# Reordering the sum and gather work around one PSUM bank, and the first and last of 64 late jobs, in a retention, GLU and expert-mixture kernel

## The chip, the cores and the metric

The kernel runs on one core of one Trainium2 chip. The metric is the device time of one execution in microseconds (us), taken as the median of several runs; lower is better. In the profile the engines are PE (TensorE matmul), PEld (TensorE's weight loads, which overlap its matmuls), DVE (VectorE), ACT (ScalarE), POOL (GpSimd) and SP (SyncE, which here issues most DMAs).

## The reference

Three layers follow each other on 2304 tokens of 512 features: a retention (attention with a decaying mask and no softmax), a gated linear unit, and a mixture of 8 experts in which every token goes through every expert, weighted by a Sinkhorn-normalized matrix. Only the last layer matters here:

```python
def _moe2_ref(x, w_gate, w1, w2):        # x 2304x512, w1 8x512x1024, w2 8x1024x512
    logits = x @ w_gate
    P = np.exp(logits - logits.max())
    for _ in range(8):
        P /= P.sum(1, keepdims=True) + 1e-09
        P /= P.sum(0, keepdims=True) + 1e-09
        P *= N / E
    out = np.zeros((N, D))
    for e in range(E):
        h = np.maximum(x @ w1[e], 0.0)
        out += P[:, e:e + 1] * (h @ w2[e])
```

Each fp32 matrix operand is split into a high part `hi` (rounded to the matmul's type) and a rest `lo = x - hi`, and each product is computed as `hi*hi + hi*lo + lo*hi`, three matmuls.

## The kernel before

**Jobs.** The mixture is cut into 96 jobs: 3 units of 768 tokens, in each unit 8 experts, and in each expert 4 groups of 256 hidden features. The 32 jobs of unit 0 also prepare the weights and keep them in DRAM. The 64 late jobs (numbers 32 to 95, units 1 and 2) load them back. All engine queues run in the order in which the program is written; nothing reorders it.

**A late job.** Both layers of a job are done by a Strassen-like scheme of 7 block products with sums of blocks (A11, A12, A22, S1 to S4) in place of 8 products. A first-layer product (`block_product`) is 6 matmuls of 128x384, into the PSUM banks `px`, `py`, `pz` or `qz`. A second-layer step (`second`) is 3 matmuls, and 7 steps for each of two output halves `j`; they go into `qx`, `qy`, `qz` and a bank `shared_sums[j]` (the tiles `pv` and `e`). So a job issues 42 + 42 = 84 matmuls.

**The order within the loop.** The body of job `n` holds the first layer of job `n`, most of the second layer of job `m = n - 1`, and the last two second-layer steps (`c12` and `c21` for `j = 1`) of job `l = n - 2`, woven together. The second layer needs the parts of the hidden blocks of `m`: `high(m, S2)` is a cast on ACT, and `low(m, S2)` a subtraction on DVE or, for S3 and S4, on POOL (line 975). The results leave PSUM by `gather`, an addition `acc += bank` on DVE (line 989); the names `add_11`, `add_22`, `add_12`, `add_21` say which quarter. `add_12` empties `qy` and `add_21` empties `qz`.

In the order of each queue, the first half of a body is:

- PE: product A11 of `n` into `px`; `c12(l, 1)` into `qy`; `c21(l, 1)` into `qz`; product S2 of `n` into `py`; `first(m, 0)` into `qx`; `shared(m, 0)` into `pv`; product S1 of `n` into `qz`; `third(m, 0)`, which reads the parts of S2, into `qy`; `c11(m, 0)`, which reads the parts of A12, into `qx`; product A12.
- DVE, from the end of the body before: `h_blocks[1]` (line 1157), `add_22(m, 1)`, `low A11`, `add_11(m, 1)`, and then `low S1`, `low A12`, `add_12(l, 1)`, `add_21(l, 1)`, `low S2`.
- POOL: the four sums S1 to S4 of the hidden blocks (lines 1152, 1154, 1173, 1174), then `low S3` and `low S4`.
- ACT: `high S1, A12, S2`, the copy `py <- px`, `high S3`, the copy `pz <- py`, the copy `qy <- qx` (line 999, which overwrites the bank that `add_12` reads), `high S4`.

**Homes of the sums.** The blocks and sums of a job lie in `h_blocks` (the tile `a22_block` and `old[:, 0, 0]`) and `sums`, four pieces of `old`. `old` is `acc_d[:, :, :768]`, the place of unit 0's output, which the six DMAs of line 811 (issued by ACT, inside `outputs_of` of job 31) write out while job 32 (`opening` in the code) already runs.

**Change of unit and end.** At job 64 the generator `switch` splits the last operands of unit 2 (line 613 on DVE, in `split`), and at job 65 `add_shared` adds the shared banks into the output of unit 1 (line 1037), after which `finish_unit` transposes it piece by piece. After the loop the last steps of jobs 94 and 95 follow, then `finish_unit` for unit 2: for each of 6 chunks of 128 tokens four transposes, a copy from PSUM to a staging tile (two of these in turn, from ACT and DVE) and an output DMA from SP.

Of the kernel before, what the change touches and what calls it, by code (L numbers as in the profile page):

```python
# [39 lines left out]
T = 384  # L40
# [9 lines left out]
def retention_glu_experts(ctx: ExitStack, tc: tile.TileContext, a, out):  # L50
# [709 lines left out]
    def block_product(n, ps, w, name, start=False):  # L760
        s = w1_slots[n % 2]
        xh, xl = x_ops[jobs[n][0]][name]
        for k in range(2):
            kc = slice(k * 128, (k + 1) * 128)
            wh, wl = s[:, 0, w, kc], s[:, 1, w, kc]
            for i, (l, r) in enumerate(((wh, xh), (wh, xl), (wl, xh))):
                nc.tensor.matmul(  # L767
                    ps, lhsT=l, rhs=r[:, k, :], start=start and k == 0 and i == 0,
                    stop=k == 1 and i == 2, skip_group_check=True,
                )  # L770
# [170 lines left out]
    old = acc_d[:, :, :UNIT].rearrange("p k (h t) -> p k h t", t=T)  # L941
    h_blocks = [a22_block, old[:, 0, 0]]
    sums = [old[:, k, h] for k, h in ((1, 0), (0, 1), (1, 1), (2, 0))]
    T1, T2, T3, T4, B21, B22, B11 = range(7)

    def halves(p, i):
# [16 lines left out]
            nc.sync.dma_start(prob_b[e % 2], prob_kept[e, (u - 1) * UNIT:u * UNIT].partition_broadcast(128))  # L963

    def operand(n, i):
        return h_ops[n % 2][i], {A22: h_blocks[0], A12: h_blocks[1], A11: z[:, 1, :]}.get(i, sums[(i - S1) % 4])

    def high(n, *parts):
        for i in parts:
            (hi, _), x = operand(n, i)  # L970
            nc.scalar.copy(hi, x)  # L971

    def low(n, i, engine=None):
        (hi, lo), x = operand(n, i)
        (engine or nc.vector).tensor_sub(lo, x, f32(hi))  # L975
# [20 lines left out]
    def first(n, j):  # L996
        x, y, z, e = banks_of(n, j)
        second(n, j, A11, B11, x, start=True)
        nc.scalar.copy(y, x)  # L999
# [15 lines left out]
    def c12(n, j):  # L1015
        second(n, j, S4, B22, banks_of(n, j)[1])

    def c21(n, j):
        second(n, j, A22, T4, banks_of(n, j)[2])
# [7 lines left out]
    def add_12(n, j):  # L1027
        gather(n, 2 + j, 1, banks_of(n, j)[1])

    def add_21(n, j):  # L1030
        gather(n, j, 0, banks_of(n, j)[2])

    def add_shared(u):
        for j in range(2):
            for h in range(2):
                o = acc_d[:, 2 + j, u * UNIT + h * T:u * UNIT + (h + 1) * T]
                nc.vector.tensor_add(o, o, shared_sums[j])

    def finish_unit(u, banks, stages):
        for t in range(NCH):  # L1040
            ps = banks[t % len(banks)]
            tag, shape = stages[t % len(stages)]
            at = u * UNIT + t * 128
            for k in range(KD):
                nc.tensor.transpose(ps[:, k * 128:(k + 1) * 128], acc_d[:, k, at:at + 128], ident)
            st = ev.tile(shape, F32, tag=tag, name=f"st{u}_{t}").rearrange("p a b -> p (a b)")[:, :DM]
            if t % len(stages):
                nc.vector.tensor_copy(st, ps)
            else:
                nc.scalar.copy(st, ps)  # L1050
            nc.sync.dma_start(out[at:at + 128, :], st)
            yield
# [3 lines left out]
    for n, (u, e, g) in list(enumerate(jobs))[UJ:]:  # L1056
        opening = n == UJ
        m, l = n - 1, n - 2
        pb = prob_b[e % 2]
        load_w1(n + 1)  # L1060
        if u + 1 < NU and (e, g) == (E - 1, NPAIR - 3):
            switch = unit_operands(u + 1)
        ahead = u + 1 < NU and (e, g) in ((E - 1, NPAIR - 3), (E - 1, NPAIR - 2))
        turn = u + 1 < NU and (e, g) == (E - 1, NPAIR - 1)
        begins = (e, g) == (0, 0)
        if g == NPAIR - 1:
            load_probs(n + 1)

        block_product(n, px, 0, "A11", start=True)
        if not opening:  # L1070
            high(m, S2)
        nc.scalar.copy(py, px)  # L1072
        if not opening:
            high(m, S3)
            low(m, S1)
            low(m, A12)
        if begins:
            next(switch)
        if l >= UJ:
            c12(l, 1)  # L1080
            c21(l, 1)
            add_12(l, 1)
            add_21(l, 1)
            if jobs[l][1:] == (E - 1, NPAIR - 1):
                add_shared(jobs[l][0])
                finishing = finish_unit(jobs[l][0], [qx_all], [("xs", [128, 2, T])])
        load_w2(n)
        p5 = ev.tile([128, T], F32, tag="p5", name=f"p5_{n}")
        if opening:
            block_product(n, pv, 3, "S1", start=True)  # L1090
            nc.scalar.copy(p5, pv)
            next(ys)
            block_product(n, py, 4, "S2")
            nc.scalar.copy(pz, py)
            next(switch)
            next(ys)
        else:
            low(m, S2)
            block_product(n, py, 4, "S2")
            nc.scalar.copy(pz, py)  # L1100
            if turn or begins:
                next(switch)
            first(m, 0)
            high(m, S4)
            low(m, S3, nc.gpsimd)
            low(m, S4, nc.gpsimd)
            shared(m, 0)
            block_product(n, qz, 3, "S1", start=True)
            nc.scalar.copy(p5, qz)
            if ahead:  # L1110
                next(switch)
            third(m, 0)
            c11(m, 0)
            add_11(m, 0)

        block_product(n, px, 1, "A12")
        nc.vector.scalar_tensor_tensor(h_blocks[0], px, 0.0, pb[:, :T], ALU.max, ALU.mult)
        if turn:
            next(switch)
        if opening:  # L1120
            next(ys)
        else:
            next(finishing, None)
            c22(m, 0)
            add_22(m, 0)
            c12(m, 0)
            add_12(m, 0)
        high(n, A22)
        low(n, A22)

        block_product(n, pz, 5, "S3")
        z = ev.tile([128, 2, T], F32, tag="z", name=f"z{n}")
        nc.vector.tensor_add(z[:, 1, :], pz, p5)  # L1133
        if turn or ahead:
            next(switch)
        if opening:
            next(ys)
        else:
            first(m, 1)
            c21(m, 0)  # L1140
            add_21(m, 0)

        block_product(n, py, 2, "S4")
        nc.vector.tensor_add(z[:, 0, :], py, p5)
        z_2 = z.rearrange("p h t -> p (h t)")
        nc.vector.scalar_tensor_tensor(z_2, z_2, 0.0, pb, ALU.max, ALU.mult)  # L1146
        if opening:
            next(ys)
        else:
            third(m, 1)  # L1150
            shared(m, 1)
        nc.gpsimd.tensor_add(sums[0], z[:, 0, :], h_blocks[0])  # L1152
        high(n, A11)
        nc.gpsimd.tensor_sub(sums[1], sums[0], z[:, 1, :])

        block_product(n, pz, 6, "A22")
        nc.vector.scalar_tensor_tensor(h_blocks[1], pz, 0.0, pb[:, T:], ALU.max, ALU.mult)
        if opening:
            for _ in ys:
                pass  # L1160
            shared_all, shared_sums = pv_all, [pv, pac.tile([128, 512], F32, tag="ac", name="e1")[:, :T]]
            qx_all, qy, qz = (pac.tile([128, 512], F32, tag="ac", name=f"q{i}") for i in "xyz")
            qx, qy, qz = (q[:, :T] for q in (qx_all, qy, qz))
            for q in (qy, qz):
                nc.tensor.matmul(q, lhsT=sx[:, 0, 0, 0, :128], rhs=sx[:, 0, 0, 0, :], start=True, stop=True)
        else:
            c22(m, 1)
            add_22(m, 1)
        low(n, A11)
        if not opening:  # L1170
            c11(m, 1)
            add_11(m, 1)
        nc.gpsimd.tensor_sub(sums[2], z[:, 1, :], z[:, 0, :])
        nc.gpsimd.tensor_sub(sums[3], h_blocks[1], sums[1])
        high(n, S1, A12)

    n, l = len(jobs) - 1, len(jobs) - 2
    high(n, S2, S3)
    low(n, S1)
    low(n, A12)  # L1180
    c12(l, 1)
    add_12(l, 1)
    first(n, 1)
    c21(l, 1)
    add_21(l, 1)
    low(n, S2)
    first(n, 0)
    high(n, S4)
    low(n, S3, nc.gpsimd)
    low(n, S4)  # L1190
    for step in (shared, third, c11):
        for j in (1, 0):
            step(n, j)
            if step is c11:
                add_11(n, j)
    add_shared(NU - 1)
    for step, add in ((c22, add_22), (c12, add_12), (c21, add_21)):
        for j in (1, 0):
            step(n, j)
            add(n, j)  # L1200
    for _ in finish_unit(NU - 1, [shared_all, qx_all, px_all, py_all], [("xs", [128, 2, T]), ("z", [128, 2, T])]):
        pass


# [69 lines left out]
```

## Time and profile before

| what | us |
|---|---|
| median of 3 runs | 2132.06 (2130.42 to 2132.81) |
| the profiled execution's own time | 2136.81 |
| its span, first to last instruction | 2134.9 |
| PE busy / PEld busy in the span | 2058.7 / 1884.9 |
| DVE / ACT / POOL busy | 1480.1 / 860.3 / 846.5 |
| mean granted TensorE clock | 0.990 |

PE counts as busy from the start of a matmul to its modelled end, and these overlap, so its share hides short waits; the waits of PEld, which come when a weight load is held back, show them better. A row of a timeline gives start, length, engine, line, operation, output and inputs, and in square brackets how long the engine had been idle and what released it. In the profile's names `z` and `a_block` and `acc` are the homes of the hidden blocks and sums, `xhi` and `xlo` those of their parts.

### The profile page before, as it was taken

To read this page: it belongs to the slowest core of one execution; us is meant where nothing else is said; L and a number is where in the kernel's file an instruction comes from. 1 tells how busy PE (TensorE), PEld (TensorE's weight loads), DVE (VectorE), ACT (ScalarE), POOL (GpSimd) and SP (SyncE) were. 2 spreads that over 40 slices of the span, in tenths; PEclk is the share of its full clock that TensorE was granted. 3 is DMA by queue.
4 is the path that set the end of the run, shared out by engine and by line. 5 is a ranking of instruction groups with operands and counts; after the bars stand their busy time and mean duration, and the time that the engine had idled before them with its cause. 6 is when DMAs were issued, how large, how long until landed. Compare 5 with 4: busy or idle time off the path is not lost.

```text
span 2134.9 us, 30383 instructions
## 1 busy us (share of the span) xinstructions
PE 2058.7 (96%) x11526; PEld 1884.9 (88%) x11526; DVE 1480.1 (69%) x2323; ACT 860.3 (40%) x1649; POOL 846.5 (40%) x747
## 2 busy tenths in 40 slices
PE   8999999999998999999998999999999999999997
PEld 5688789889777899999998999999998999999997
DVE  6863775653579777777785777777776677777776
ACT  3443322221353544444444444444445444444443
POOL 3421542210043445555443353444464444444443
PEclk8999999999999999999999999999999999999999
DMA  6420220100056888888877666666665767666763
GB/s 219 158 87 1 79 70 30 60 30 1 1 197 252 290 295 306 310 300 307 301 282 294 245 253 245 250 248 247 251 236 221 273 230 272 223 258 232 270 227 129
DMA packets 112690, 436.58 MB, mean 204 GB/s; under 512 B 12297, under 2 KB 30473, under 8 KB 96161
## 3 DMA queue, kind: packets, MB, share of 16 engines
q1 hardware_dynamic: 110048, 432.72, 55.4%
q10 hardware_dynamic: 2496, 1.94, 0.3%
q8 instruction: 90, 1.47, 0.3%
q14 instruction: 56, 0.45, 0.1%
HBM read 312.40 MB, written 122.21 MB: 204 GB/s over the span
## 4 chain that ended last, share of the span: by engine, by line
PE 71%; DVE 20%; ACT 1%; DMA 1%; issue 1%; POOL 0%; DVEq 0%; SPq 0%; POOLq 0%; ACTq 0%
PE pz L767 9%; DVE xlo L975 9%; PE py L767 6%; PE px L767 6%; DVE acc L989 6%; PE qy L981 5%; PE gv L173 4%; PE gv L175 4%; PE gv L174 4%; PE qz L767 4%; PE y L174 4%; PE y L175 4%; PE y L173 4%; PE qx L981 3%; PE qz L981 3%; PE x L173 2%
## 5 line engine op out<-in xcount | busy, mean ns | idle before, releaser
L1152 POOL TENSOR_TENSOR acc<-z,a_block 128x384 f32<-128x384 f32 x64 | 64.9, 1015 | 509.2 <-DVE z L1146 481.7
L767 PE MATMUL py<-sx,w1s 128*128 128x384 f32 x1152 | 233.0, 337 | 6.0 <-ACT py L1072 5.8
L767 PEld LDWEIGHTS py<-sx,w1s 128*128 128x128 f32 x1152 | 203.7, 188 | 10.0 <-ACT py L1072 7.3
L767 PE MATMUL px<-xhi,w1s 128*128 128x384 f32 x640 | 188.9, 335 | 0.0
L971 ACT CAST xhi<-acc 128x384 fp32r<-128x384 f32 x320 | 158.1, 514 | 74.6 <-POOL acc L1152 35.4
L975 DVE TENSOR_TENSOR xlo<-acc,xhi 128x384 fp32r<-128x384 f32 x193 | 178.1, 949 | 2.7 <-ACT xhi L971 2.6
L975 POOL TENSOR_TENSOR xlo<-acc,xhi 128x384 fp32r<-128x384 f32 x127 | 148.9, 1172 | 43.6 <-ACT xhi L971 43.6
L989 DVE TENSOR_TENSOR acc<-acc,qz 128x384 f32<-128x384 f32 x246 | 134.7, 547 | 25.7 <-PE qz L981 25.6
L989 DVE TENSOR_TENSOR acc<-acc,qx 128x384 f32<-128x384 f32 x123 | 67.3, 547 | 118.1 <-PE qx L981 118.1
L576 POOL TENSOR_TENSOR t<-rw 128x256 f32<-128x256 f32 x32 | 47.0, 1467 | 238.9 <-issue 126.9
L121 POOL TENSOR_SCALAR cv<-raw 128x512 f32<-128x512 f32 x36 | 63.2, 1758 | 182.0 <-DVE wslots L143 91.6
L174 PE MATMUL gv<-xlo,wslots 128*128 128x512 f32 (+2 forms) x368 | 126.8, 345 | 3.0 <-DVE xlo L407 1.7
L173 PE MATMUL gv<-xhi,wslots 128*128 128x512 f32 (+2 forms) x368 | 127.9, 347 | 0.4 <-ACT xhi L404 0.4
L175 PE MATMUL gv<-xhi,wslots 128*128 128x512 f32 (+2 forms) x368 | 126.4, 343 | 0.0
L809 DVE SCALAR_TENSOR_TENSOR acc<-y,prob,acc 128x512 f32<-128x512 f32 x168 | 118.0, 741 | 7.9 <-PE y L175 7.9
L201 DVE TENSOR_TENSOR t<-t,gv 128x512 f32<-128x512 f32 (+2 forms) x66 | 38.8, 588 | 115.9 <-PE gv L175 115.9
L767 PEld LDWEIGHTS px<-xhi,w1s 128*128 128x128 f32 x640 | 118.3, 188 | 0.4
L767 PE MATMUL pz<-sx,w1s 128*128 128x384 f32 x576 | 115.6, 335 | 0.0
L767 PE MATMUL pz<-xhi,w1s 128*128 128x384 f32 x384 | 113.8, 336 | 1.5 <-DVE z L1133 1.0
L999 ACT COPY qy<-qx 128x384 f32<-128x384 f32 x127 | 58.8, 463 | 127.0 <-PE qx L981 89.9
L767 PE MATMUL px<-xlo,w1s 128*128 128x384 f32 x320 | 107.1, 335 | 0.0
L175 PE MATMUL y<-xlo,xhi 128*128 128x512 f32 x264 | 103.8, 393 | 0.0
(360 smaller groups left out, 6067.1 us busy)
## 6 DMA issues: line engine op xcount, KB each, us to landing
w1s<-w_kept SPq DMA_DIRECT2D x64, 1792.0 KB, 7.1
w_kept<-w1s SPq DMA_DIRECT2D x32, 1792.0 KB, 6.6
rw<-in_w_dram SPq DMA_DIRECT2D x64, 512.0 KB, 5.4
w_kept<-xlo SPq DMA_DIRECT2D x64, 512.0 KB, 3.7
w2s<-w_kept SPq DMA_DIRECT2D x32, 1024.0 KB, 7.0
w_extra<-w_kept SPq DMA_DIRECT2D x32, 768.0 KB, 7.7
w_kept<-xlo SPq DMA_DIRECT2D x44, 384.0 KB, 4.2
w2c<-w_kept SPq DMA_DIRECT2D x32, 512.0 KB, 7.9
```

The source lines that it names most:

```text
L121: nc.gpsimd.tensor_scalar(sign, high_f, -least, None, ALU.is_le)
L173: nc.tensor.matmul(ps, lhsT=lh, rhs=rh, start=start, stop=False)
L174: nc.tensor.matmul(ps, lhsT=lh, rhs=rl, start=False, stop=False)
L175: nc.tensor.matmul(ps, lhsT=ll, rhs=rh, start=False, stop=stop)
L767: nc.tensor.matmul(ps, lhsT=l, rhs=r[:, k, :], start=start and k == 0 and i == 0, stop=k == 1 and i == 2, skip_group_check=True,)
L809: nc.vector.scalar_tensor_tensor(o, y_2, pe, o, ALU.mult, ALU.add)
L971: nc.scalar.copy(hi, x)
L975: (engine or nc.vector).tensor_sub(lo, x, f32(hi))
L981: nc.tensor.matmul(ps, lhsT=l, rhs=r, start=start and i == 0, stop=i == 2, skip_group_check=True)
L989: nc.vector.tensor_add(dst, dst, ps)
L999: nc.scalar.copy(y, x)
L1152: nc.gpsimd.tensor_add(sums[0], z[:, 0, :], h_blocks[0])
```

## The change

In the loop, `low(m, A12)` moves from ahead of the gathers of job `l` to behind `low(m, S2)`, and `add_21(l, 1)` goes ahead of `add_12(l, 1)`. The matmuls keep their order. In the opening job the blocks and sums get other homes: a staging tile `xs`, the tile `prob_b[1]` (not loaded until job 35) and, for the last of them alone, `old[:, 0, 0]`. After the loop the last steps are put in another order, `low S3` goes from POOL to DVE, and `add_shared` is split between the gathers. The chunks of a unit are written out from the last to the first; for unit 2 there are six banks and six staging tiles in place of four and two.

```diff
+    homes = h_blocks, sums
...
     def operand(n, i):
-        return h_ops[n % 2][i], {A22: h_blocks[0], A12: h_blocks[1], A11: z[:, 1, :]}.get(i, sums[(i - S1) % 4])
+        blocks, sums = opening_homes if n == UJ else homes
+        return h_ops[n % 2][i], {A22: blocks[0], A12: blocks[1], A11: z[:, 1, :]}.get(i, sums[(i - S1) % 4])
...
-    def add_shared(u):
-        for j in range(2):
-            for h in range(2):
+    def add_shared(u, *js):
+        for j in js:
+            for h in (1, 0):
...
-    def finish_unit(u, banks, stages):
-        for t in range(NCH):
-            ps = banks[t % len(banks)]
-            tag, shape = stages[t % len(stages)]
+    def finish_unit(u, banks, stages=None):
+        for i, t in enumerate(reversed(range(NCH))):
+            ps = banks[i % len(banks)]
...
-            st = ev.tile(shape, F32, tag=tag, name=f"st{u}_{t}").rearrange("p a b -> p (a b)")[:, :DM]
-            if t % len(stages):
+            if stages:
+                st = stages[i]
+            else:
+                st = ev.tile([128, 2, T], F32, tag="xs", name=f"st{u}_{t}").rearrange("p a b -> p (a b)")[:, :DM]
+            if i % 2 and stages:
                 nc.vector.tensor_copy(st, ps)
             else:
                 nc.scalar.copy(st, ps)
...
         if not opening:
             high(m, S3)
             low(m, S1)
-            low(m, A12)
         if begins:
             next(switch)
+        if opening:
+            xs = ev.tile([128, 2, T], F32, tag="xs", name="opening_sums")
+            opening_homes = [a22_block, prob_b[1][:, :T]], [xs[:, 0, :], xs[:, 1, :], prob_b[1][:, T:], old[:, 0, 0]]
+        h_blocks, sums = opening_homes if opening else homes
         if l >= UJ:
             c12(l, 1)
             c21(l, 1)
+            add_21(l, 1)
             add_12(l, 1)
-            add_21(l, 1)
...
         else:
             low(m, S2)
+            low(m, A12)
             block_product(n, py, 4, "S2")
...
     n, l = len(jobs) - 1, len(jobs) - 2
-    high(n, S2, S3)
+    high(n, S2)
     low(n, S1)
+    c21(l, 1)
+    c12(l, 1)
+    add_21(l, 1)
+    first(n, 1)
+    add_12(l, 1)
+    first(n, 0)
+    high(n, S3)
+    low(n, S2)
     low(n, A12)
-    c12(l, 1)
-    add_12(l, 1)
-    first(n, 1)
-    c21(l, 1)
-    add_21(l, 1)
-    low(n, S2)
-    first(n, 0)
+    low(n, S3)
     high(n, S4)
-    low(n, S3, nc.gpsimd)
     low(n, S4)
-    for step in (shared, third, c11):
+    for step in (shared, third, c11, c22, c12):
         for j in (1, 0):
             step(n, j)
-            if step is c11:
-                add_11(n, j)
-    add_shared(NU - 1)
-    for step, add in ((c22, add_22), (c12, add_12), (c21, add_21)):
+    for add in (add_11, add_22, add_12):
         for j in (1, 0):
-            step(n, j)
             add(n, j)
-    for _ in finish_unit(NU - 1, [shared_all, qx_all, px_all, py_all], [("xs", [128, 2, T]), ("z", [128, 2, T])]):
+            if add is add_22:
+                add_shared(NU - 1, j)
+    for j in (1, 0):
+        c21(n, j)
+    for j in (1, 0):
+        add_21(n, j)
+    stages = [
+        ev.tile([128, 2, T], F32, tag="xs", name="st_xs").rearrange("p a b -> p (a b)"), old[:, 3].rearrange("p h t -> p (h t)"),
+        prob_b[0], acc_d[:, 1, :UNIT], z.rearrange("p h t -> p (h t)"), prob_b[1],
+    ]
+    for _ in finish_unit(NU - 1, [shared_all, px_all, qx_all, py_all, qy_all, shared_1], [t[:, :DM] for t in stages]):
         pass
```

## Rows read from the trace of the kernel before

**Rows 1.** Waits of PEld from 1165 to 2111 us: total us, times, longest.

```profile
PEld qz L767 <- DVE acc L989: 48.1, 59, 2.3
```

**Rows 2.** Timeline, DVE line 1157, once a job: jobs 34, 63 and 64.

```profile
1167.16 0.56 DVE L1157 SCALAR_TENSOR_TENSOR acc<-pz,prob_b 128x384 f32<-128x384 f32 x1 [0.60 <-PE pz L767]
...
1611.39 0.55 DVE L1157 SCALAR_TENSOR_TENSOR acc<-pz,prob_b 128x384 f32<-128x384 f32 x1
...
1630.52 0.56 DVE L1157 SCALAR_TENSOR_TENSOR acc<-pz,prob_b 128x384 f32<-128x384 f32 x1 [0.60 <-PE pz L767]
```

**Rows 3.** Timeline of PEld in job 60: loads of products S2 and S1.

```profile
1552.72 1.05 PEld L767 LDWEIGHTS py<-sx,w1s 128*128 128x128 f32 x6
...
1555.61 1.01 PEld L767 LDWEIGHTS qz<-x_more,w1s 128*128 128x128 f32 x6 [0.80 <-DVE acc L989]
```

**Rows 4.** Timeline of DVE in the same job: low S1, A12, gathers, low S2.

```profile
1552.44 0.91 DVE L975 TENSOR_TENSOR xlo<-acc,xhi 128x384 fp32r<-128x384 f32 x1
...
1553.27 1.37 DVE L975 TENSOR_TENSOR xlo<-acc,xhi 128x384 fp32r<-128x384 f32 x1
1554.56 0.54 DVE L989 TENSOR_TENSOR acc<-acc,qy 128x384 f32<-128x384 f32 x1
1555.02 0.54 DVE L989 TENSOR_TENSOR acc<-acc,qz 128x384 f32<-128x384 f32 x1
1555.48 0.54 DVE L975 TENSOR_TENSOR xlo<-acc,xhi 128x384 fp32r<-128x384 f32 x1
```

**Rows 5.** Timelines of POOL and ACT in the same job.

```profile
1554.18 1.32 POOL L975 TENSOR_TENSOR xlo<-acc,xhi 128x384 fp32r<-128x384 f32 x1
1556.15 1.01 POOL L975 TENSOR_TENSOR xlo<-acc,xhi 128x384 fp32r<-128x384 f32 x1 [0.65 <-ACT xhi L971]
...
1555.18 0.46 ACT L999 COPY qy<-qx 128x384 f32<-128x384 f32 x1 [0.59 <-DVE acc L989]
1555.56 0.52 ACT L971 CAST xhi<-acc 128x384 fp32r<-128x384 f32 x1
```

**Rows 6.** Timelines of DVE and POOL at the seam of jobs 33 and 34.

```profile
1154.12 1.39 DVE L975 TENSOR_TENSOR xlo<-acc,xhi 128x384 fp32r<-128x384 f32 x1 [0.87 <-ACT xhi L971]
...
1154.08 1.02 POOL L1173 TENSOR_TENSOR acc<-z 128x384 f32<-128x384 f32 x1
```

**Rows 7.** Timeline of PEld in job 65, first load of `shared(m, 0)`.

```profile
1637.00 0.29 PEld L981 LDWEIGHTS pv<-xhi,w2s 128*128 128x128 f32 x1 [2.23 <-DVE acc L1037]
```

**Rows 8.** Busy time by stretch: us, PE, PEld, DVE, ACT, POOL, granted clock, DMA share, GB/s.

```profile
700.00:800.00 100.00, 100.00 (x509) 90.35 (x509) 71.50 (x94) 46.55 (x70) 48.89 (x51) 1.00 0.82 296
...
1620.00:1624.00 4.00, 4.00 (x15) 3.98 (x15) 1.04 (x2) 0.94 (x2) 1.35 (x1) 0.58 0.49 195
...
1636.00:1640.00 4.00, 3.00 (x9) 3.00 (x10) 2.35 (x6) 0.53 (x2) 1.00 (x1) 0.63 0.97 382
```

**Rows 9.** Timelines of DVE, ACT and PEld at the opening job.

```profile
1134.17 0.56 DVE L1157 SCALAR_TENSOR_TENSOR acc<-pz,prob_b 128x384 f32<-128x384 f32 x1 [2.03 <-DMA out_dram<-acc]
...
1132.76 0.51 ACT L971 CAST xhi<-z 128x384 fp32r<-128x384 f32 x1 [4.45 <-DVE acc L809]
1135.42 0.54 ACTq L811 DMA_DIRECT2D out_dram<-acc  x1
1136.00 0.92 ACT L971 CAST xhi<-acc 128x384 fp32r<-128x384 f32 x2 [2.73 <-DVE xlo L975]
1137.99 0.51 ACT L971 CAST xhi<-acc 128x384 fp32r<-128x384 f32 x1 [1.06 <-POOL acc L1154]
...
1138.93 0.82 PEld L767 LDWEIGHTS py<-sx,w1s 128*128 128x128 f32 x3 [5.64 <-ACT py L1072]
```

**Rows 10.** Timelines of DVE and ACT from the last gather to the end.

```profile
2123.61 0.54 DVE L989 TENSOR_TENSOR acc<-acc,qz 128x384 f32<-128x384 f32 x1
...
2131.19 0.69 DVE L1048 COPY st<-qx 128x512 f32<-128x512 f32 x1 [2.17 <-DMA out_dram<-st]
...
2127.63 0.59 ACT L1050 COPY st<-px 128x512 f32<-128x512 f32 x1 [2.15 <-DMA out_dram<-st]
```

More of the change, by code (lines that the diff above doesn't have):

```diff
@@ L1081, in retention_glu_experts @@
             c21(l, 1)
+            add_21(l, 1)
             add_12(l, 1)
-            add_21(l, 1)
             if jobs[l][1:] == (E - 1, NPAIR - 1):
-                add_shared(jobs[l][0])
-                finishing = finish_unit(jobs[l][0], [qx_all], [("xs", [128, 2, T])])
+                add_shared(jobs[l][0], 0, 1)
+                finishing = finish_unit(jobs[l][0], [qx_all])
         load_w2(n)
@@ L1160, in retention_glu_experts @@
                 pass
-            shared_all, shared_sums = pv_all, [pv, pac.tile([128, 512], F32, tag="ac", name="e1")[:, :T]]
-            qx_all, qy, qz = (pac.tile([128, 512], F32, tag="ac", name=f"q{i}") for i in "xyz")
-            qx, qy, qz = (q[:, :T] for q in (qx_all, qy, qz))
+            shared_all, shared_1, qx_all, qy_all, qz = (pv_all, *(pac.tile([128, 512], F32, tag="ac", name=n) for n in ("e1", "qx", "qy", "qz")))
+            shared_sums = [pv, shared_1[:, :T]]
+            qx, qy, qz = (q[:, :T] for q in (qx_all, qy_all, qz))
             for q in (qy, qz):
```

## The prediction, on record before the change was built

> **What bounds the kernel now.** I read the waits first, since the shares mislead: TensorE counts as busy for 2058.7 of 2134.9 us. In the waits of its weight loads one group holds nearly everything: the loads of product S1 into bank `qz` are held 59 times, 48.1 us in all, by the gather on DVE [rows 1]. That is once in every late job from 34 on, except in 65 and in the few jobs whose gathers run on ACT. One of them is the 2.3 us of job 64, so the other 58 take 45.8 / 58 = 0.79 us each.
>
> Next the pitch of the jobs: DVE's line 1157 comes at 1167.16 in job 34 and at 1611.39 in job 63 [rows 2], 444.23 / 29 = 15.318 us a job. What would it be without the wait? Six loads take 1.05 us with the last one's overlap, and the next group follows 1.04 us after the first load, 0.1734 each [rows 3]; 84 of them are 14.562. So the wait costs 15.318 - 14.562 = 0.756 us a job.
>
> Then the timeline of DVE, to see why the gather is late. `low A12` takes 1.37 us and the gather of `qy` 0.46 before the gather of `qz` starts at 1555.02 [rows 4]. Neither is needed yet by TensorE. The load that waits started at 1555.61 after 0.80 of idleness [rows 3], so it could have gone at 1554.81.
>
> **The loop.** Nothing is added; two subtractions and two gathers on DVE change places. I lay out job 60 with the durations of its rows. `low S1` ends at 1553.35 as before [rows 4]. An instruction of DVE starts up to 0.08 before the one ahead ends, so the gather of `qz` starts at 1553.27 and ends at 1553.81. The product it waits for, `c21(l, 1)`, ends before product S2, whose loads begin at 1552.72 [rows 3], has got far: its last matmul ends about 0.33 after that, at 1553.05, so the gather, now ahead in the queue, is not held, by 0.2 us. TensorE wants `qz` at 1554.81: the wait is gone with a margin of 1 us. The gather of `qy` follows at 1553.73 and `low S2` at 1554.19, with the spacing of 0.46 seen between gathers [rows 4].
>
> What is late next is `low A12`. Its reader is the second load of `c11(m, 0)`, ten loads after 1554.81 (six of S1, three of `third`, one): 1556.54. The price of the two subtractions is what I must bound. Without POOL at work one takes 0.54 [rows 4]; with POOL at work 0.91 and 1.37 [rows 4], or 1.39 [rows 6]. Splitting the time evenly could at most double 0.54 to 1.08, so these rows show one engine standing still while the other works: in [rows 6] POOL starts 0.04 us earlier and DVE ends 0.41 after POOL's end. So whoever starts first is taken first. POOL's `low S3` starts at 1554.18 [rows 5], 0.01 ahead of DVE's `low S2`; I price `low S2` like [rows 6], 1.39: it ends at 1555.58 (were DVE first, at about 1554.65). Its reader, the second load of `third(m, 0)`, comes at 1554.81 + 7 x 0.1734 = 1556.02; that holds. `low A12` then starts at 1555.50. POOL's `low S4` follows ACT's cast of S4. That cast is behind the copy `qy <- qx`, held for 0.59 by the gather of `qy` until 1555.18 [rows 5]; this gather is now 0.83 earlier, so the copy can move up to at most 1554.59, the cast to 1554.97 and its end to 1555.49, and POOL, 0.07 behind, to 1555.56. That is 0.06 to 0.1 us after DVE's start: DVE goes first, `low A12` ends at 1556.05, and TensorE is not held, by 0.4 us. POOL's `low S4` then ends near 1556.95; it is read by `c12(m, 0)`, whose loads come at 1554.81 + 21 x 0.1734 = 1558.45.
>
> [...]
>
> The loads move earlier, but for DMA nothing changes: same order, same issue points behind TensorE. So 58 jobs x 0.756 = 43.8 us; with up to 0.05 of leftover wait a job, 41.
>
> **Change of unit.** Job 64 takes 1630.52 - 1611.39 = 19.13 us [rows 2]. [...] The change brings the gather of `qz` one gather forward (0.46), and takes `low A12` from POOL's way (up to 0.3). The wait becomes about 1.5 to 1.85. After the waits of 0.8 no fall of the clock is seen, after 2.23 one is (0.63 over four microseconds [rows 7, 8]). I take that 1.5 is short enough: 0.8 + 1.4 = 2.2 us, between 0.5 and 2.4. In job 65 TensorE waits 2.23 us for `add_shared` [rows 7]; of what stood ahead of it, `low A12` (1.37) goes behind, so 1.0 is left, as in a steady job before, where the clock held: 1.27 + 1.5 (4 x 0.37 [rows 8]) = 2.8, between 1.2 and 2.8.
>
> **Opening.** TensorE stands still for 5.64 us before product S2 of job 33 [rows 9]. Two chains lead there: DVE's line 1157 waits 2.03 until the output DMA has left `old`, and the output DMA issued by ACT waits behind it until 1135.42; and POOL's sums wait for the same DMAs, so the cast of S2 comes at 1137.99 [rows 9]. With the new homes both are free. ACT's cast of A11 ends at 1133.27. DVE's line 1157 can start 2.03 earlier, 1132.14, and the last output DMA, which ACT issued 1.25 after it, about 1133.4. From there it takes the DMA issue (0.54), the casts of S1 and A12 (0.92), of S2 (0.51) [rows 9] and the copy (0.46 [rows 5]), less overlaps of about 0.1: 1135.7 in place of 1138.93. That saves 3.2 us and leaves a wait of 2.4, after which I expect the clock to fall as it does now. If it holds, some 1.5 more; if the weights that job 32 loads land later than needed, up to 0.9 less. The last sum keeps `old`, but its turn on POOL comes after 1134.2, when line 1157 shows the DMA gone.
>
> **End.** From the end of the last gather, 2124.15, to the end of the span at 2134.9 are 10.75 us. The six copies go through two staging tiles, and the second and third of each wait 2.15 to 2.3 for the DMA of the one before [rows 10]. With six tiles there are three copies on ACT (0.59) and three on DVE (0.69), side by side, 2.1 us; with the transposes ahead of the first, put at 0.6, the last ends 2.7 us after the last gather, instead of at 2131.88, 7.73 after it: 5.0 less. The six DMAs then overlap and may hold each other up by 0.8. `low A12` (1.37) no longer stands ahead of `low S2` of job 95, so the chain of steps behind it can begin up to 1.3 earlier. Together 5.0 - 0.8 + 1.3 = 5.5, between 4.5 and 6.3. `low S3` costs DVE one more 0.54 and takes POOL out of its way.
>
> **Sum.** 43.8 + 2.2 + 2.8 + 3.2 + 5.5 = 57.5 us. The profiled execution took 2136.81, so 2079.3 in its terms; the median of the runs stands 4.75 below it, 2132.06 - 57.5 = 2074.5.
>
> **Rivals.** *POOL goes first.* If POOL's `low S4` starts before DVE's `low A12`, which decides within 0.1 us, DVE stands still until POOL is done: 1555.6 + 1.01 + 0.41 = 1557.03, and TensorE waits 1557.09 - 1556.54 = 0.55 a job, 32 us: 2106.5. For it speaks the small margin, against it the order in [rows 6]. [...] I give it 0.10. *The wait moves.* If another of TensorE's waits stands right behind `qz` (the copy of `qy`, the parts of S2), the loop keeps most of its 0.756 and only 13.7 us come from the ends: 2118. Against it: the margins of 0.4 us and more above. 0.08, partial cases (2085 to 2100) among them. *The clock.* [...] 0.03.
>
> **How the numbers follow.** My forecast has 0.79; its own range, from the bounds of its terms (loop 41 to 44, unit 1.7 to 5.2, opening 2.3 to 4.7, end 4.5 to 6.3), is 49.5 to 60.2 us, 2072 to 2082.6, with the spread of the runs 2070 to 2084. To hold 8 in 10, the range takes in the partial cases: 2069 to 2100. About 0.2% (4 us) can be told from no change; all cases but the clock's lie beyond it: faster 0.96, same 0.01, slower 0.03.
>
> **What would show it.** Right: no wait of PEld for `qz` in the loop; line 1157 every 14.56 us; `low S2` at 1.39 and `low A12` at 0.54; job 65 without a fall of the clock; a wait near 2.4 at the opening; no copy at the end waiting for a DMA. Wrong: a wait of `c11` for `low A12`, or a pitch above 14.7.

## The result and the profile after

The changed kernel takes 2075.35 us (median of 4 runs, 2073.81 to 2078.93) beside 2132.43 for the kernel before on the same chip (2130.42 to 2133.68): a ratio of 0.9736, with a 95% interval of 0.9719 to 0.9752. The profiled execution took 2074.04 us, its span is 2072.1.

First the page of the changed kernel: span, the granted clock in 40 slices of it (tenths of full speed; 9 is 90% or more), and the chain of work that ended last.

```profile
span 2072.1 us, 30381 instructions
...
PEclk9999999999999999999999999999999999999999
...
PE 89%; DVE 7%; ACT 2%; DMA 1%; issue 1%; POOL 0%; SPq 0%; ACTq 0%; DVEq 0%; POOLq 0%
```

TensorE now carries 89% of the chain (71% before), and the clock shows no slice below 0.9. The waits of PEld from 1100 us to the end (total us, times, longest) are to be set beside [rows 1]:

```profile
PEld py L767 <- ACT py L1076: 4.2, 5, 2.4
PEld qz L767 <- DVE acc L991: 1.5, 1, 1.5
...
PEld pv L983 <- DVE acc L1039: 0.9, 1, 0.9
...
PEld qx L983 <- DVE xlo L977: 0.6, 1, 0.6
```

Of the 59 waits for the gather out of `qz` one is left, that of job 64. DVE's line that writes `h_blocks[1]`, now 1165, gives the pitch (jobs 34, 63, 64 and 65), as [rows 2] did:

```profile
1157.86 0.56 DVE L1165 SCALAR_TENSOR_TENSOR acc<-pz,prob_b 128x384 f32<-128x384 f32 x1 [0.60 <-PE pz L767]
...
1580.91 0.55 DVE L1165 SCALAR_TENSOR_TENSOR acc<-pz,prob_b 128x384 f32<-128x384 f32 x1
...
1597.73 0.56 DVE L1165 SCALAR_TENSOR_TENSOR acc<-pz,prob_b 128x384 f32<-128x384 f32 x1 [0.60 <-PE pz L767]
...
1613.81 0.56 DVE L1165 SCALAR_TENSOR_TENSOR acc<-pz,prob_b 128x384 f32<-128x384 f32 x1 [0.60 <-PE pz L767]
```

(1580.91 - 1157.86) / 29 = 14.588 us a job in place of 15.318, and most single jobs take 14.56. The timelines of DVE, POOL and PEld in one such job answer to [rows 3 to 5]. From the top: `low S1`, the gathers of `qz` and `qy`, `low S2`, `low A12`; POOL's `low S3` and `low S4`; the loads of S1, of the matmul in `third` that reads the low part, and of that in `c11`:

```profile
1524.26 0.91 DVE L977 TENSOR_TENSOR xlo<-acc,xhi 128x384 fp32r<-128x384 f32 x1
1525.09 0.54 DVE L991 TENSOR_TENSOR acc<-acc,qz 128x384 f32<-128x384 f32 x1
1525.55 0.54 DVE L991 TENSOR_TENSOR acc<-acc,qy 128x384 f32<-128x384 f32 x1
1526.02 1.41 DVE L977 TENSOR_TENSOR xlo<-acc,xhi 128x384 fp32r<-128x384 f32 x1
1527.35 0.55 DVE L977 TENSOR_TENSOR xlo<-acc,xhi 128x384 fp32r<-128x384 f32 x1
...
1526.00 1.01 POOL L977 TENSOR_TENSOR xlo<-acc,xhi 128x384 fp32r<-128x384 f32 x1
1527.44 1.32 POOL L977 TENSOR_TENSOR xlo<-acc,xhi 128x384 fp32r<-128x384 f32 x1 [0.43 <-ACT xhi L973]
...
1526.62 1.05 PEld L767 LDWEIGHTS qz<-x_more,w1s 128*128 128x128 f32 x6
...
1527.84 0.19 PEld L983 LDWEIGHTS qy<-xlo,w_extra 128*128 128x128 f32 x1
...
1528.36 0.19 PEld L983 LDWEIGHTS qx<-xlo,w_extra 128*128 128x128 f32 x1
```

None of the three loads waits. The gather of `qz` is over at 1525.63, 0.99 us ahead of its reader; `low S2` at 1527.43, 0.41 ahead; `low A12` at 1527.90, 0.46 ahead. POOL starts 0.02 ahead of `low S2`, which then takes 1.41 us; DVE starts 0.09 ahead of POOL's `low S4`, and `low A12` takes 0.55.

One job went the other way, number 62. Its `low A12` on DVE, `low S4` on POOL and the second load of `c11`:

```profile
1556.80 1.37 DVE L977 TENSOR_TENSOR xlo<-acc,xhi 128x384 fp32r<-128x384 f32 x1
...
1556.73 1.03 POOL L977 TENSOR_TENSOR xlo<-acc,xhi 128x384 fp32r<-128x384 f32 x1 [0.26 <-ACT xhi L973]
...
1558.23 0.19 PEld L983 LDWEIGHTS qx<-xlo,w_extra 128*128 128x128 f32 x1 [0.57 <-DVE xlo L977]
```

POOL is 0.07 ahead, `low A12` takes 1.37, and TensorE waits 0.57; this job takes 15.28 us. It is the rival "POOL goes first", once; in the 56 steady jobs DVE is 0.09 to 0.11 ahead.

At the change of unit, two waits of PEld (job 64 for the gather, job 65 for `add_shared`) answer to [rows 7]:

```profile
1587.94 0.19 PEld L767 LDWEIGHTS qz<-xhi,w1s 128*128 128x128 f32 x1 [1.52 <-DVE acc L991]
...
1602.93 0.19 PEld L983 LDWEIGHTS pv<-xhi,w2s 128*128 128x128 f32 x1 [0.94 <-DVE acc L1039]
```

The stretches behind them (us, busy of PE, PEld, DVE, ACT, POOL, granted clock, DMA share, GB/s) answer to [rows 8]:

```profile
1590.00:1600.00 10.00, 10.00 (x59) 10.00 (x59) 7.68 (x14) 3.91 (x9) 3.75 (x4) 1.00 0.31 96
1600.00:1615.00 15.00, 14.38 (x84) 13.84 (x83) 9.34 (x17) 8.05 (x18) 5.51 (x6) 1.00 0.66 249
```

The clock stays at 1.00. At the opening, DVE's line 1165 and the load of product S2 of job 33 answer to [rows 9]:

```profile
1127.46 0.55 DVE L1165 SCALAR_TENSOR_TENSOR prob_b<-pz,prob_b 128x384 f32<-128x384 f32 x1
...
1131.05 1.01 PEld L767 LDWEIGHTS py<-sx,w1s 128*128 128x128 f32 x6 [2.37 <-ACT py L1076]
```

And the stretch behind that load:

```profile
1132.00:1136.00 4.00, 4.00 (x25) 4.00 (x24) 1.40 (x2) 2.75 (x6) 1.99 (x2) 1.00 1.08 436
```

Line 1165 no longer waits for a DMA, the load waits 2.37 us in place of 5.64, and the clock stays at 1.00 here too. Last the end (DVE: last gather, last copy; ACT: first and second copy; SP: last DMA issue), for [rows 10]:

```profile
2064.93 0.55 DVE L991 TENSOR_TENSOR acc<-acc,qz 128x384 f32<-128x384 f32 x1
...
2067.26 0.69 DVE L1052 COPY prob_b<-e 128x512 f32<-128x512 f32 x1 [0.18 <-PE e L1046]
...
2065.07 0.58 ACT L1054 COPY st_xs<-pv 128x512 f32<-128x512 f32 x1 [5.43 <-PE pv L1046]
2065.94 0.58 ACT L1054 COPY prob_b<-qx 128x512 f32<-128x512 f32 x1 [0.29 <-PE qx L1046]
...
2068.17 0.60 SPq L1055 DMA_DIRECT2D out_dram<-prob_b  x1
```

No copy waits for a DMA; the last ends 2.47 us after the last gather.

Now the span, cut at the line that writes `h_blocks[1]` and at the row of `z <- py` in job 32. That row before and after:

```profile
1129.95 0.54 DVE L1144 TENSOR_TENSOR z<-py,p 128x384 f32<-128x384 f32 x1
...
1125.35 0.55 DVE L1152 TENSOR_TENSOR z<-py,p 128x384 f32<-128x384 f32 x1
```

Each stage is the difference of two such rows. Jobs 34 and 66 are left out; they take the same time in both kernels to 0.04.

| stage | before | after | gain | the prediction's term |
|---|---|---|---|---|
| opening, `z` row to job 33 | 22.28 | 17.54 | 4.74 | 3.2 |
| jobs 35 to 63 | 444.23 | 423.05 | 21.18 | 21.9 |
| job 64 | 19.12 | 16.82 | 2.30 | 2.2 |
| job 65 | 18.80 | 16.08 | 2.72 | 2.8 |
| jobs 67 to 95 | 445.98 | 424.05 | 21.93 | 21.9 |
| end, from job 95's row | 24.21 | 18.87 | 5.34 | 5.5 |
| sum | | | 58.21 | 57.5 |

The spans differ by 62.8 us. The other 4.6 lie ahead of job 32's `z` row, in code that the change leaves alone; over all profiles of this study that row lies between 1125.35 and 1130.91, whatever the kernel.

### The profile page after: what moved, and what is told of

It is laid out like the page before. It is cut to its first block, busy times and chain, and to the rows that moved or that the text cites. A ratio compares the mean times of both kernels' runs of the same rounds, so it can differ in the third digit from the quotient of the medians.

```text
span 2072.1 us, 30381 instructions
## 1 busy us (share of the span) xinstructions
PE 2033.0 (98%) x11526; PEld 1880.2 (91%) x11526; DVE 1483.8 (72%) x2324; ACT 860.0 (42%) x1649; POOL 844.0 (41%) x746
## 3 DMA queue, kind: packets, MB, share of 16 engines
q8 instruction: 90, 1.47, 0.3%
## 4 chain that ended last, share of the span: by engine, by line
PE 89%; DVE 7%; ACT 2%; DMA 1%; issue 1%; POOL 0%; SPq 0%; ACTq 0%; DVEq 0%; POOLq 0%
PE py L767 9%; PE pz L767 9%; PE px L767 9%; PE qy L983 6%; PE qx L983 6%; PE qz L983 6%; PE gv L173 5%; PE gv L174 4%; PE gv L175 4%; PE y L174 4%; PE y L175 4%; PE y L173 4%; PE qz L767 3%; PE x L173 2%; PE x L174 2%; PE x L175 2%
## 5 line engine op out<-in xcount | busy, mean ns | idle before, releaser
L175 PE MATMUL y<-xlo,xhi 128*128 128x512 f32 x264 | 103.8, 393 | 0.0
L174 PE MATMUL y<-xlo,xhi 128*128 128x512 f32 x264 | 103.8, 393 | 0.0
```

What stands on the lines that cost most here:

```text
L174: nc.tensor.matmul(ps, lhsT=lh, rhs=rl, start=False, stop=False)
L175: nc.tensor.matmul(ps, lhsT=ll, rhs=rh, start=False, stop=stop)
```

## The experiments

The theory: the gain comes from the waits for `qz` in the loop, and it holds because DVE starts `low A12` just ahead of POOL's `low S4`. The rivals: POOL's start order does not matter (the two engines share the time, or slack), or the gain is that of one edit alone, or the clock gives it.

**The loop alone.** Only the two edits of the loop are made:

```diff
             low(m, S1)
-            low(m, A12)
...
-            add_12(l, 1)
             add_21(l, 1)
+            add_12(l, 1)
...
             low(m, S2)
+            low(m, A12)
```

> The kernel before with the loop's change alone: low A12 behind low S2, and the gather of qz ahead of that of qy; opening and end as before. Theory (the wait for bank qz was the loss in the loop): no wait of PEld for qz in a steady job, 14.56 us from job to job in place of 15.32, 58 x 0.756 = 43.8 us, and 5.0 us in jobs 64 and 65: 2132.4 - 48.8 = 2083.6, with the opening's wait of 5.6 us and the last 24.2 us as before. Rival (the gain came from the new homes and the end): less than 15 us gained, 2117 or more.

Measured: 2087.91 us, ratio 0.9785 [0.9768, 0.9801], by that ratio 45.9 us of 2134.84; 48.8 were expected, which the interval, 42.5 to 49.5, still holds. By the stages jobs 35 to 63 take 423.05 us and jobs 67 to 95 424.05, as in the full change to the last digit shown; jobs 64 and 65 take 16.77 and 16.07. The opening stays at 22.37 and the end at 24.22. So the loop edits give 48.2 us of the profile, the units' jobs among them.

The clock does not give it. In the kernel before, the two long stretches of jobs without a change of unit (columns as above) were granted 1.00 as well:

```profile
1167.16:1611.39 444.23, 430.61 (x2438) 421.25 (x2437) 329.32 (x527) 194.09 (x410) 207.61 (x178) 1.00 0.67 248
1646.00:2110.00 464.00, 450.25 (x2557) 440.49 (x2556) 337.27 (x538) 202.53 (x432) 207.21 (x180) 1.00 0.65 243
```

**Each loop edit alone.** One kernel only exchanges the two gathers, another only moves `low A12`.

> The kernel before with only the two gathers changed in order; low A12 still ahead of both. Theory (the time of the gather of qz on DVE is all that counts): it comes one gather, 0.46 us, earlier, so 0.3 of the 0.76 us a job is left: 15.32 - 0.46 = 14.86 from job to job, 58 x 0.46 + 0.5 = 27 us, 2105. Rival (putting qz first is what frees TensorE, and the place of low A12 does not matter): 14.56, 2084.

> The kernel before with only low A12 moved behind low S2; the gather of qy still ahead of that of qz. Theory: the gather of qz ends 0.46 us later than in the full change, at 1554.27 of the time axis of the kernel before, still 0.5 us ahead of the load at 1554.81, so the steady job takes 14.56 us as with both; only job 64, where the split stands ahead of the gathers, loses 0.46 or, with a fall of the clock, 2 us: 2084 to 2086. Rival (qz has to be first): a wait of 0.3 us or more is left, 14.9 from job to job, 2101 or more.

Measured: 2107.48, 0.9874 [0.9859, 0.9888] for the exchange; 2086.96, 0.9777 [0.9763, 0.9792] for the move. The waits of the exchange and a load of S1 in one of its jobs:

```profile
PEld qz L767 <- DVE acc L989: 20.8, 58, 1.8
...
1540.84 1.00 PEld L767 LDWEIGHTS qz<-x_more,w1s 128*128 128x128 f32 x6 [0.34 <-DVE acc L989]
```

The exchange brings the gather one gather forward (0.46) and leaves 0.34 of the wait of 0.80 in [rows 3]; its jobs take 14.87. With the move alone the jobs take 14.56, as with both. In the loop the move is the whole gain. The exchange counts only in job 64, where the gather is still late: 16.82 with both, 17.26 with the move alone, a difference of 0.44.

**`low A12` made later than POOL.** Three fills of a small tile that nothing reads stand ahead of it, each 0.07 us on DVE. As a control the same fills stand behind it.

```diff
             low(m, S2)
+            for i in range(3):
+                nc.vector.memset(small.tile([128, TT, 1], F32, tag="r", name=f"late{n}_{i}"), 0.0)
             low(m, A12)
```

> The changed kernel with three fills of 128x18 elements of a scratch tile on DVE between low S2 and low A12 of each job; nothing reads them. They push the start of low A12 back by about 0.2 us, behind the start of POOL's low S4, which came 0.09 us after it. Theory (whoever starts first is taken first, and the margin is the 0.09 us): low A12 stands still until POOL is done, takes about 1.3 us, and c11 waits 0.55 us in each job: 15.1 from job to job, 62 x 0.55 = 34 us more than the changed kernel, 2109. Rival (DVE and POOL share, or DVE goes first anyway): low A12 ends 0.2 us later, still ahead of c11, 14.56 from job to job, 2075.

> Control for the run that pushed low A12 back: the same three fills of a scratch tile on DVE, but behind low A12. Theory (what cost 30 us was POOL starting ahead of low A12): low A12 starts ahead of POOL as in the changed kernel, 14.56 us from job to job, 2075. Rival (the fills themselves, or their waits, cost the time): 15.1, 2104.

Measured: 2103.98, 0.9863 [0.9849, 0.9878] with the fills ahead; 2077.36, 0.9729 [0.9716, 0.9743] with them behind, beside 0.9734 of the unaltered change on that chip. Waits with the fills ahead, and one job's `low A12`, POOL's `low S4` and the load of `c11`:

```profile
PEld qx L983 <- DVE xlo L977: 31.1, 57, 0.6
...
1526.32 1.36 DVE L977 TENSOR_TENSOR xlo<-acc,xhi 128x384 fp32r<-128x384 f32 x1
...
1526.25 1.01 POOL L977 TENSOR_TENSOR xlo<-acc,xhi 128x384 fp32r<-128x384 f32 x1 [0.43 <-ACT xhi L973]
...
1527.73 0.19 PEld L983 LDWEIGHTS qx<-xlo,w2s 128*128 128x128 f32 x1 [0.55 <-DVE xlo L977]
```

The fills shift DVE from 0.09 ahead of POOL to 0.07 behind (0.05 to 0.08 in the 57 jobs). The subtraction then takes 1.36 in place of 0.55, and `c11` waits 0.55 in 57 jobs: 31.1 us, where the prediction's rival said 0.55 a job and 32. Its length cannot be the fills' own, since behind `low A12` they cost nothing. So for these two subtractions who starts first decides, as the theory has it.

**The two subtractions the other way round.** `low A12` goes ahead of `low S2`, both still behind the gathers.

```diff
-            low(m, S2)
             low(m, A12)
+            low(m, S2)
```

> The changed kernel with low A12 ahead of low S2, both behind the gathers. Theory: the first of the two is taken behind POOL's low S3 and ends 1.4 us after its start, the second 0.46 later; now that is low S2, whose reader, third, comes 0.52 us ahead of c11, so it is about 0.05 to 0.1 us late: 14.56 to 14.65 from job to job, 2075 to 2081. If POOL's low S4 slips in ahead of low S2, the wait is about 1.05 us: 15.6, 2140. Rival (nothing hangs on which is first, as both are ready in time): 14.56, 2075.

Measured: 2081.21, 0.9761 [0.9748, 0.9774]. A job takes 14.61. The loads of `third` in one of them:

```profile
1536.10 0.19 PEld L983 LDWEIGHTS qy<-xhi,w_extra 128*128 128x128 f32 x1
1536.37 0.19 PEld L983 LDWEIGHTS qy<-xlo,w_extra 128*128 128x128 f32 x1
```

0.27 lies between the two in place of 0.17. The long subtraction is now that of A12 (POOL starts 0.01 ahead of it; the two of DVE take 1.88 together), and `low S2`, second, ends just after its reader could go; half of the 0.1 is caught up behind it: 0.05 a job. Over both stages it is 3.5 us (2.0 and 1.5), 0.5 of them in job 62, which takes 15.74. Jobs 64 and 65 add 0.6, and a fall of the clock at the opening 1.5 (below). The order of the two in the change is the better one, by little.

**Opening alone, end alone.** One kernel adds only the other homes of job 32, the other is the change without loop and opening.

> The kernel before with only the opening job's blocks and sums in their new homes. [...]

> The kernel before with only the last steps after the loop and the writing out of the units changed (six banks, six staging tiles, last chunk first). Theory: from DVE's line that writes h_blocks[1] in job 95 to the end of the span 18.8 us in place of 24.2, 5.4 gained: 2127.0. Rival (the output DMAs themselves set the end, so more tiles only make them wait for each other): 22 us or more, 2130 or more.

Measured: 2126.99, 0.9969 [0.996, 0.9978], and 2127.97, 0.9976 [0.9967, 0.9985]. The opening stage takes 17.51 in the first and the end 18.87 in the second, as in the full change. By the ratios the three parts give 2.15%, 0.31% and 0.24%, together 2.70% beside 2.64% for the whole: within their intervals they add up. The load of product S2 in job 33 waits 2.39 in the first, in place of 5.64. The opening gives 6.6 us by its ratio, where the prediction has 3.2, or 4.7 if the clock holds, and its stage gives 4.8, near the lower end of its interval (4.7 to 8.5); what the rest is was not settled.

The first held a surprise. Nothing in it touches jobs 64 and 65, yet they take 17.57 and 17.25 us in place of 19.12 and 18.80. The wait of job 64 in this kernel, from PEld's timeline:

```profile
1614.63 0.19 PEld L767 LDWEIGHTS qz<-xhi,w1s 128*128 128x128 f32 x1 [2.32 <-DVE acc L991]
```

The stretch that begins with it, in the columns above:

```profile
1614.00:1618.00 4.00, 3.37 (x19) 3.37 (x20) 2.47 (x5) 1.83 (x4) 1.62 (x1) 1.00 0.83 341
```

The wait is the 2.3 of the kernel before, but the clock stays at 1.00, where [rows 8] shows 0.58. In the kernel with the end alone it falls in job 64, behind the same wait, and not in job 65, as the two stretches there show:

```profile
1614.00:1618.00 4.00, 3.25 (x11) 3.25 (x12) 2.03 (x4) 1.72 (x4) 1.60 (x1) 0.66 0.86 352
1632.00:1636.00 4.00, 3.45 (x20) 3.46 (x21) 1.89 (x5) 1.50 (x4) 1.01 (x1) 1.00 1.00 384
```

**The waits that are left at the change of unit.** One kernel takes the split of `switch` from ahead of the gathers to behind `low A12`; a second also splits `add_shared` in job 65, `j = 0` ahead of the gathers and `j = 1` behind `low A12` (its edit, which holds the first kernel's, is shown). The third is the change unaltered, on the same chip as the second.

```diff
-        if begins:
+        if opening:
             next(switch)
...
             c21(l, 1)
+            if jobs[l][1:] == (E - 1, NPAIR - 1):
+                add_shared(jobs[l][0], 0)
             add_21(l, 1)
             add_12(l, 1)
             if jobs[l][1:] == (E - 1, NPAIR - 1):
-                add_shared(jobs[l][0], 0, 1)
...
             low(m, A12)
+            if l >= UJ and jobs[l][1:] == (E - 1, NPAIR - 1):
+                add_shared(jobs[l][0], 1)
+            if begins:
+                next(switch)
```

> The changed kernel with the split that stands ahead of the gathers in job 64 moved behind low A12 of that job. Theory (the 1.5 us that TensorE still waits for qz in job 64 come from this split): that wait goes, job 64 takes 15.3 us in place of 16.8, 1.5 less in the profile and 2074 in the runs, less than the runs can tell. Rival (the casts on ACT hold the job up): 16.5 us or more.

> The changed kernel with the split of job 64 behind low A12, and in job 65 the shared bank that TensorE wants first added ahead of the two gathers, the other behind low A12. Theory: the 1.5 us wait of job 64 and the 0.9 us wait of job 65 both go; job 64 takes 15.3 and job 65 15.1 us, 2.5 less than the changed kernel, 2073. Rival (the wait of job 65 moves to qz, to the copy of qy or to the parts of S2): job 65 stays at 15.6 or more.

> The changed kernel once more, unaltered, beside the kernel before and the two below on one chip. Both theories: 2075, 0.9736 of the kernel before; its profile shows how far the time ahead of job 32, which the change does not touch, and a fall of the clock at the opening differ from one execution to another. A theory that these belong to the change expects the opening job to begin near 1125 us again and the clock to hold.

Measured: 2074.08, 0.9724 [0.971, 0.9737] with the split late; 2073.16, 0.9711 [0.9697, 0.9724] with `add_shared` split too (2071.98 to 2074.42); 2077.72, 0.9734 [0.972, 0.9747] unaltered (2076.27 to 2079.43). Job 64 falls from 16.80 to 15.33, and in the second kernel job 65 from 16.06 to 15.07. In the second kernel one wait of PEld of more than 0.1 us is left between 1580 and 1612 us, that is in these two jobs:

```profile
1585.62 1.01 PEld L767 LDWEIGHTS py<-sx,w1s 128*128 128x128 f32 x6 [0.78 <-ACT py L1076]
```

So the two waits of 1.52 and 0.94 were on the path: without them the jobs take 1.47 and 0.99 less. The second kernel is the fastest here, and all its runs lie below all of the unaltered change on that chip. Its median lies 4.6 us lower, of which these two jobs explain 2.5; of the 3.9 between the profiles, 1.3 lies ahead of job 32. Whether the change has a part in more than the 2.5 stays open.

## Why the prediction held, step by step

The forecast was 2074.5, the median is 2075.35. Term by term, with the table above:

**The loop, 43.8; measured 43.1.** "The wait is gone with a margin of 1 us": 0.99. `low S2` at 1.39 and `low A12` at 0.54: 1.41 and 0.55. "TensorE is not held, by 0.4 us": 0.46. The pitch of 14.56 is that of most jobs. The 0.7 us that lack are job 62, which the prediction counted as a steady job: in job 61 the next unit's preparation begins on DVE, ACT and POOL, and in job 62 POOL was 0.07 ahead. It is no accident of one execution: in all seven profiles with `low A12` last and nothing ahead of it, job 62 takes 15.26 to 15.31. That the preparation shifts the order is a reading of the timelines; no run tests it. The step "That is 0.06 to 0.1 us after DVE's start: DVE goes first" held in the steady jobs at 0.09, and the late subtraction shows what it was worth: 29.1 us over the two stages (436.92 + 439.26 beside 423.05 + 424.05).

Two runs show the same subtraction at 0.55 with DVE 0.09 ahead (the change) and at 1.36 with DVE 0.07 behind (the late subtraction). By what means POOL holds DVE up was not shown.

**Job 64, 2.2; measured 2.30.** "The wait becomes about 1.5 to 1.85": 1.52. The step "I take that 1.5 is short enough" for the clock held in this profile and in the five others with a wait of 1.5. No run shows the 1.4 that its sum puts for the fall of the clock; they show 1.55, job 64 of the kernel before (19.12) beside job 64 with the same wait and no fall (17.57).

**Job 65, 2.8; measured 2.72.** "1.0 is left": 0.94, with the clock at 1.00. In its sum 1.27 stands for the shorter wait, where 2.23 - 1.0 is 1.23; the slip changes little.

That these two terms came out so well is in part luck. 1.4 and 1.5 of them are falls of the clock that the one profile of the kernel before happened to have. The kernel with the opening alone has the same two waits without the falls and takes 17.57 and 17.25; beside such an execution the change gains 0.75 and 1.17 in the two jobs, not 2.30 and 2.72.

**Opening, 3.2; measured 4.74.** The wait came as worked out, 2.37 for 2.4, and it is the step behind it that failed: "after which I expect the clock to fall as it does now". It did not fall, and the 1.5 that the prediction set aside for that case came on top. Eight profiles have this wait of 2.36 to 2.39 us: in six the clock holds and the stage takes 17.5, in two it falls and the stage takes 19.1. The forecast of this term was the rarer case.

**End, 5.5; measured 5.34.** From the end of the last gather (2065.48) to the end of the span are 6.6 us in place of 10.75: 4.1, where the prediction had 5.0 - 0.8 = 4.2. Within it the copies gained more, 5.3 (the last ends 2.47 after the last gather in place of 7.73), and the DMAs behind them cost more: from the end of the last copy to the end of the span are 4.15 in place of 3.02, that is 1.1 where the prediction put 0.8, a figure that no row showed. The rest, 1.2, is the shorter chain ahead of it, put at 1.3: the wait of `third` for `low S2` falls from 1.4 to 0.4 there. The other steps changed places too, and what each gave was not separated.

**The rivals.** "POOL goes first" does occur, once in job 62 (`low A12` at 1.37) and made on purpose in 57 jobs (1.36); the change stands on the other side of it by 0.09 us. "The wait moves" did not come: no new wait in the loop apart from job 62. "The clock" did not come either. From job 32 to the last gathers TensorE was busy for 930 of 935 us and granted 1.00:

```profile
1125.00:2060.00 935.00, 930.00 (x5354) 926.11 (x5355) 721.18 (x1142) 433.64 (x921) 447.25 (x386) 1.00 0.69 258
```

The medians differ by 57.1 us, the stages of the two profiles by 58.2. Falls of the clock that come in some executions only (1.5 us each, below) and the varying time ahead of job 32 are both large enough for the rest; their shares in it were not measured. So the loop, three quarters of the sum, was forecast by its mechanism; that the whole came within 0.9 us was luck too. The misses of the opening and the loop have opposite signs, and the prediction took gains read in a profile of 2136.81, with three falls of the clock from the opening on, off a median of 2132.06.

## What to carry to other kernels

Read the waits of the weight loads, not the busy share of TensorE, and look in the queue of the engine that is waited for, at what stands ahead of the needed instruction without being needed yet. Moving the long one of these behind (0.756 a job) was worth more than bringing the needed one a single place forward (0.45). Then price the moved instruction at its new place against its neighbour on POOL (0.55 or 1.36 here), and ask how near the order of the two starts is: here a shift of 0.16 us cost 27 of the 57 us gained. And take a second profile before a fall of the clock enters a sum: seen once, it is a property of that execution, not yet of the kernel.

## What the runs showed of the hardware that was not expected

**The same wait, with and without a fall of the clock.** Behind waits of TensorE of 2.2 to 2.4 us the granted clock fell in some executions and stayed at 1.00 in others. In job 64 of the kernel before it was 0.50 from 1620 to 1623 us, and the weight loads there follow each other by 0.32 in place of 0.17. At the opening it fell in 2 of 8 profiles, in jobs 64 and 65 in 3 of 7 cases; behind the waits of 5.6 us of the old opening in 5 of 5, behind 1.5 to 2.0 in none. A fall costs 1.5 to 1.6 us in the stage. The opening of the kernel with the two subtractions exchanged, 19.07 for the 17.5 of the others, begins with this load of PEld:

```profile
1136.61 1.00 PEld L767 LDWEIGHTS py<-sx,w1s 128*128 128x128 f32 x6 [2.36 <-ACT py L1076]
```

The two stretches of 4 us from there:

```profile
1136.00:1140.00 4.00, 3.39 (x13) 3.39 (x14) 2.95 (x3) 2.35 (x6) 2.57 (x3) 0.71 1.10 419
1140.00:1144.00 4.00, 4.00 (x21) 4.00 (x21) 0.32 (x1) 1.42 (x3) 0.97 (x1) 0.86 0.98 408
```

What decides between the two was not settled.

**An unchanged part that varies.** The time from the start to job 32 differs by up to 5.6 us between profiles (1125.35 to 1130.91), more than the whole effect of the opening or of the change of unit. It does not belong to the kernel: the unaltered change begins job 32 at 1125.35 in one profile and at 1127.97 in the other. Single spans can't be compared at that size. Stages of the same code, cut at the same instruction, agree to 0.1 us where the clock does the same; the old opening is the exception, with 22.11 to 22.37 and once 23.08.
